# One x tile instead of two transposed on TensorE; the second comes first through the DMA transpose, behind the loads of Wk

## The chip, the cores and the metric

The kernel runs on one core of one Trainium2 chip. A core has five engines that run side by side: TensorE (PE, the matmuls; its weight loads stand in the profile as PEld), VectorE (DVE), ScalarE (ACT), GpSimd (POOL) and SyncE (SP, which here only issues transfers). Transfers run on 16 DMA engines that all queues share; SP and ACT each have a queue of their own. The metric is the device time of one execution in microseconds (us), and lower is better. A profile shows the span from the first instruction to the last; a little time lies around it.

## The reference

A block of linear attention with 32 heads of 20 columns, sequence length 2048, width 640, in bf16:

```python
B, S, D = 1, 2048, 640;  H = 32;  Dh = D // H
q, k, v = split(x @ wqkv)                  # wqkv: 640 x 1920, each part (B, H, S, Dh)
phi = lambda t: where(t > 0, t + 1, exp(t)) + 1e-6
pq, pk = phi(q), phi(k)
kv  = einsum("bhsd,bhse->bhde", pk, v)     # summed over the sequence, per head
z   = einsum("bhsd->bhd", pk)
num = einsum("bhqd,bhde->bhqe", pq, kv)
den = einsum("bhqd,bhd->bhq", pq, z)[..., None] + 1e-6
out = (num / den).reshape(B, S, D) @ wo
```

## The kernel before

The sequence is cut into 16 tiles of 128 rows, the width into 5 chunks of 128 columns. Wk is the middle third of `wqkv`; its 5 row chunks of 160 KB are `wk` chunks 0 to 4. The work goes in this order on TensorE: a few warm-up matmuls on constants; K = x Wk, tile by tile (line 293); the product of pk with x, from which kv is made with Wv later (line 317, "P"); Q in blocks of 512 rows (line 354), mixed with P; the small products that fold kv and Wo into one matrix; the denominators; the output (line 576).

A matmul needs x with its columns on the partitions. So there are two copies of x in SBUF: `xn`, rows on partitions, as it lies in memory (used by P and by the transposes), and `xT`, transposed (used by K and Q). `xT` is filled in two ways. Tiles below `NPE` are loaded into `xn` and turned on TensorE by `transpose_x`: five 128x128 transposes in two parts (chunks 0 and 1, then 2 to 4) into a PSUM bank each, copied out by VectorE (first part, line 212) and ScalarE (second part, line 209). All other rows come by DMA transposes (`load_xT`, line 189), one for each entry of `XCH` from number `NPE` on, all issued by SP. Before the change `NPE` is 2, and the entries used are rows 256 to 384, 384 to 640, 640 to 1024, 1024 to 1536 and 1536 to 2048: tile 2, tiles 3 and 4, 5 to 7, 8 to 11, 12 to 15.

One K tile is ten matmuls of 320 columns: two halves (`h`) of five chunks, accumulated in two PSUM banks (`k_half`). Four tiles use the eight banks in turn, so tile 4 needs the banks of tile 0. `k_phi` then runs one ScalarE exponential (line 306) and two VectorE operations (lines 308 and 311) for each tile.

`Plan` writes out one list of instructions for each engine, in the order of the program, and puts a semaphore wait ahead of an instruction where it reads what another engine or a transfer wrote. Nothing is reordered: an engine that waits holds up all that stands behind it. Loads go out in this order before the change (a letter and two numbers name a range of chunks or tiles: `w23` is `wk` chunk 2, `x12` is tile 1 of `xn`):

- SP: the left half of x tile 0, w01, w23, w34; then the five DMA transposes; then `load_rest`: Wq, x rows for tiles 2 to 7, 8 to 11, 12 to 15, ten pieces of Wv, three of Wo.
- ACT: the exponential's table, the right half of x tile 0, x12, w12, w45.

At the start TensorE takes tiles 0 and 1 together, chunk by chunk as Wk lands. The order is written out by hand at line 630: `k00a` is tile 0, chunk 0, first half; `t1b` is the second part of the transpose of tile 1; `k13` is tile 1, chunk 3, both halves. From tile 2 on each tile is done whole.

Of the kernel before, what the change touches and what calls it, by code (L numbers as in the profile page):

```python
# [84 lines left out]
def bass_standalone__linear_attn_block__prompt_kernel(nc, x, wqkv, wo, out):  # L85
# [4 lines left out]
    NT = S // 128  # L90
# [10 lines left out]
    with contextlib.ExitStack() as ctx:  # L101
# [43 lines left out]
        def two_banks(b, n=HALF, parts=128):  # L145
            return ps[0:parts, BK * b:BK * b + 2 * BK].rearrange(
                "p (g j) -> p g j", j=BK)[:, :, 0:n]

        def fold(ap, j=HALF):
            return ap.rearrange("p (g j) -> p g j", j=j)  # L150
# [26 lines left out]
                    band(bm[:, GT * t:GT * (t + 1)], [[-DH if lo else DH, 3], [0, DH]],  # L177
                         -64 * t if lo else DH - 1 + 64 * t, 1 if lo else -1, "bm")

        NPE = 2  # L180
        XCH = [(0, 128), (128, 256),
               (256, 384), (384, 640), (640, 1024), (1024, 1536), (1536, 2048)]

# [3 lines left out]
        def load_xT():  # L187
            for i, (a, b) in enumerate(XCH[NPE:]):
                P.add("sp", lambda e, a=a, b=b: e.dma_start_transpose(
                    xT[:, :].rearrange("p (c s) -> p c s", s=S)[:, :, a:b], x[0, a:b, :]),  # L190
                    writes=[("xT", NPE + i)], dma=True)

# [22 lines left out]
        def xT_keys(a, b, cs=range(NC_)):  # L215
            keys = []
            for i, (p, q) in enumerate(XCH):
                if p < b and a < q:
                    keys += [("xT", i)] if i >= NPE else sorted(
                        {("xT", i, 0 if c < 2 else 2) for c in cs})  # L220
            return keys

        def w_cols(dst, lo, hi, col, key, eng):
            P.add(eng, lambda e: e.dma_start(
                dst[:, 0:NC_ * D].rearrange("p (c n) -> p c n", n=D)[:, :, lo:hi],
                wqkv[:, col + lo:col + hi].rearrange("(c p) n -> p c n", p=128)),
                writes=[key], dma=True)

        def load_xn(a, b, eng):
            P.add(eng, lambda e: e.dma_start(  # L230
                xn[:, a * D:b * D].rearrange("p (t n) -> p t n", n=D),
                x[0, 128 * a:128 * b, :].rearrange("(t p) n -> p t n", p=128)),
                writes=[("xn", t) for t in range(a, b)], dma=True)

        def load_wk():
            tl = mybir.InstLoadActFuncSet(
                name=nc.get_next_instruction_name(),
                act_func_set_id=ACT_TABLE_SET_LN_EXP, ins=[], outs=[])
            P.add("act", lambda e: e.add_instruction(tl), writes=["table"])
            for eng, lo in (("sp", 0), ("act", HALF)):  # L240
                P.add(eng, lambda e, lo=lo: e.dma_start(
                    xn[:, lo:lo + HALF], x[0, 0:128, lo:lo + HALF]),
                    writes=[("xn", 0, lo)], dma=True)
            for eng, what in (("sp", "w01 w23 w34"), ("act", "x12 w12 w45")):
                for k in what.split():
                    a, b = int(k[1]), int(k[2])
                    if k[0] == "x":
                        load_xn(a, b, eng)
                    else:
                        P.add(eng, lambda e, a=a, b=b: e.dma_start(  # L250
                            wk[:, a * D:b * D].rearrange("p (c n) -> p c n", n=D),
                            wqkv[128 * a:128 * b, D:2 * D].rearrange("(c p) n -> p c n", p=128)),
                            writes=[("wk", c) for c in range(a, b)], dma=True)
# [3 lines left out]

        def load_rest():
            w_cols(wqn, 0, D, 0, "wqn", "sp")
            for a, b in ((2, 8), (8, 12), (12, 16)):  # L260
                load_xn(a, b, "sp")
            for g, n in ((0, 5), (5, 1)):
                f = min(GT, gsz[g])
                k = gsz[g] // f * n
                for d in range(NC_):
                    P.add("sp", lambda e, g=g, f=f, k=k, d=d: e.dma_start(
                        wv[:, 128 * NG * d:128 * NG * (d + 1)].rearrange(
                            "p (j f) -> p j f", f=64)[:, 2 * g:2 * g + k, 0:f],
                        wqkv[128 * d:128 * (d + 1), 2 * D + goff[g]:2 * D + goff[g] + k * f].rearrange(
                            "p (j f) -> p j f", f=f)),  # L270
                        writes=[("wv", i, d) for i in range(g, g + n)], dma=True)
            for t in range(2):
                P.add("sp", lambda e, t=t: e.dma_start(
                    wog[64 * t:64 * t + GT, 0:5 * D].rearrange("p (g n) -> p g n", n=D),
                    wo[0:5 * GW, :].rearrange("(g t p) n -> t p g n", t=2, p=GT)[t]),
                    writes=[("wog", g, t) for g in range(5)], dma=True)
            P.add("sp", lambda e: e.dma_start(
                wog[0:gsz[5], 5 * D:6 * D], wo[goff[5]:, :]),
                writes=[("wog", 5, 0)], dma=True)

        def warm(n, cols=BK):
            for _ in range(n):
                P.add("pe", lambda e: e.matmul(  # L283
                    bank(4, cols), nc.const_aps.tensor(1.0, [128, 128], BF16),
                    nc.const_aps.tensor(1.0, [128, cols], BF16), start=True, stop=True),
                    writes=[("bank", 4)])

        def k_half(st, h, cs=range(NC_)):
            b = 2 * (st % 4)

            def mm(e):
                for c in cs:
                    r = e.matmul(  # L293
                        bank(b + h, HALF),
                        xT[:, c * S + 128 * st:c * S + 128 * st + 128],
                        wk[:, c * D + HALF * h:c * D + HALF * (h + 1)],
                        start=(c == 0), stop=(c == NC_ - 1))
                return r
            P.add("pe", mm, reads=xT_keys(128 * st, 128 * st + 128, cs) + [("wk", c) for c in cs],
                  writes=[("bank", b + h)])  # L300

        def k_phi(st):
            b = 2 * (st % 4)
            banks = [("bank", b), ("bank", b + 1)]
            t = ek[st % 3]
            P.add("act", lambda e: e.activation(fold(t[:, :]), two_banks(b), ACTF.Exp),  # L306
                  reads=banks + ["table"], writes=[("ek", st % 3)])
            P.add("dve", lambda e: e.tensor_scalar(  # L308
                t[:, :], t[:, :], 1.0, 1e-6, ALU.min, ALU.add),
                reads=[("ek", st % 3)], writes=[("ek", st % 3)])  # L310
            P.add("dve", lambda e: e.scalar_tensor_tensor(  # L311
                fold(pk[:, st * D:(st + 1) * D]), two_banks(b), 0.0, fold(t[:, :]),
                ALU.max, ALU.add),
                reads=banks + [("ek", st % 3)], writes=[("pk", st)])
# [305 lines left out]

        pool_const()
        load_wk()
        load_xT()
        load_rest()
        warm(5)
        warm(1, 128)
        for part in range(2):
            transpose_x(0, part)
        warm(1)
        order = "k00a t1a k00b t1b k10 k01 k11 k02 k12 k03 k13 k04 k14"  # L630
        for k in order.split():
            st, part = int(k[1]), "ab".find(k[-1])
            if k[0] == "t":
                transpose_x(st, part)
            else:
                for h in range(2) if part < 0 else (part,):
                    k_half(st, h, (int(k[2]),))
        for st in range(2):
            k_phi(st)
        for st in range(2, NT):  # L640
            k_half(st, 0)
            k_half(st, 1)
            k_phi(st)
# [117 lines left out]
```

## Time and profile before

| | before |
|---|---|
| time of three runs, median (lowest to highest) | 99.58 us (99.29 to 100.04) |
| the profiled execution: its time | 99.56 us |
| the profiled execution: span | 98.3 us |
| TensorE busy | 95.1 us (97%) |
| VectorE, ScalarE, GpSimd busy | 63.7, 48.8, 4.7 us |
| K (line 293): 160 matmuls | 22.8 us |
| transposes on TensorE (line 200): 10 | 1.1% of the chain that ended last |
| first and last DMA transpose issued at | 2.65 and 11.60 us |
| Wq issued at, x for tiles 2 to 7 issued at | 15.00, 16.33 us |
| first Q matmul on the chain | 29.18 us |

Times inside the execution are microseconds from the start of the span. In a timeline a row is a run of equal instructions: start, length, engine, line, operation, what it writes and reads, count, and in brackets the idle time of its engine just before and what ended it. "SPq" and "ACTq" are the queues that issue transfers; the length there is that of the issue, not of the transfer. A row of transfers gives the size in KB and the time from the start of the issue to the landing. A busy TensorE can be one that runs slowly or overlaps: starts of successive matmuls tell its pace better than their durations, which overlap.

### The profile page before, as it was taken

The numbers are of one execution on the slowest core, as the hardware profiler recorded it, in microseconds if no ns is written. First come the engines' busy times: TensorE is split into PE (matmuls) and PEld (weight loads), VectorE is DVE, ScalarE is ACT, GpSimd is POOL, SyncE is SP. The second block draws the span as 40 slices with busy tenths as digits, with TensorE's granted clock in tenths as the row PEclk, the third lists the DMA queues.
The fourth block names the chain that finished last, engine by engine and source line by source line (L and its number), as shares of the span: only waits on it lengthen the run. The fifth ranks groups of instructions, "written<-read, shape, count | busy, mean of one in ns | idle before, by whom it ended". The sixth has DMA issues, their size and how long they took to land.

```text
span 98.3 us, 1814 instructions
## 1 busy us (share of the span) xinstructions
PE 95.1 (97%) x694; PEld 61.2 (62%) x699; DVE 63.7 (65%) x124; ACT 48.8 (50%) x93; POOL 4.7 (5%) x19
## 2 busy tenths in 40 slices
PE   6999999999999999999999999999999999999991
PEld 2467777777755444445687867655557677777771
DVE  5314998888899439997839836758999206272222
ACT  5116455544526120005806456796988765453532
POOL 6500000000000000000000520000000000000000
DMA  2999999999998294000340023313200335532334
GB/s 48 320 269 194 238 157 111 350 366 360 316 169 108 21 239 80 0 0 0 63 77 7 0 63 93 94 32 86 79 0 0 133 74 168 205 117 87 130 133 137
DMA packets 26369, 12.60 MB, mean 128 GB/s; under 512 B 18553, under 2 KB 26361, under 8 KB 26361
## 3 DMA queue, kind: packets, MB, share of 16 engines
q1 hardware_dynamic: 25640, 11.87, 50.2%
q10 hardware_dynamic: 720, 0.61, 1.9%
q8 instruction: 5, 0.08, 0.3%
q14 instruction: 4, 0.02, 0.1%
HBM read 5.90 MB, written 2.62 MB: 87 GB/s over the span
## 4 chain that ended last, share of the span: by engine, by line
PE 95%; ACT 2%; issue 0%
PE ps L293 23%; PE ps L576 22%; PE ps L354 22%; PE ps L317 21%; PE ps L283 3%; ACT w2g L483 2%; PE ps L445 1%; PE ps L544 1%; PE ps L200 1%; PE ps L472 1%; ACT osb L599 0%
## 5 line engine op out<-in xcount | busy, mean ns | idle before, releaser
L317 PE MATMUL ps<-pk,xn 128*128 128x480 bf16 (+1 forms) x160 | 23.2, 299 | 0.0
L293 PE MATMUL ps<-wk,xT 128*128 128x320 bf16 x160 | 22.8, 303 | 0.0
L354 PE MATMUL ps<-xT,wqn 128*128 128x512 bf16 x95 | 22.0, 379 | 0.4 <-issue 0.2
L576 PE MATMUL ps<-w2p,pq 128*128 128x320 bf16 (+2 forms) x170 | 22.1, 291 | 0.0
L293 PEld LDWEIGHTS ps<-wk,xT 128*128 128x128 bf16 x160 | 15.6, 98 | 6.8 <-DMA wk<-in_wqkv_dram 0.9
L576 PEld LDWEIGHTS ps<-w2p,pq 128*128 128x128 bf16 x170 | 15.9, 98 | 6.2 <-issue 0.2
L317 PEld LDWEIGHTS ps<-pk,xn 128*128 128x128 bf16 x160 | 13.6, 98 | 9.4 <-issue 0.3
L362 ACT ACTIVATE eq<-ps 128x512 bf16<-128x512 f32 x20 | 11.9, 597 | 13.8 <-PE ps L354 13.6
L354 PEld LDWEIGHTS ps<-xT,wqn 128*128 128x128 bf16 x100 | 11.5, 118 | 9.1 <-issue 0.3
L306 ACT ACTIVATE ek<-ps 128x640 bf16<-128x640 f32 x16 | 11.2, 704 | 10.7 <-PE ps L293 10.1
L599 ACT CAST osb<-ps 128x320 bf16<-128x320 f32 (+2 forms) x27 | 11.0, 413 | 9.7 <-PE ps L576 9.0
L311 DVE SCALAR_TENSOR_TENSOR pk<-ps,ek 128x640 bf16<-128x640 f32 x16 | 13.2, 825 | 0.5
L569 DVE TENSOR_TENSOR pq<-pq,rd 128x512 bf16<-128x512 bf16 x20 | 7.3, 418 | 4.2 <-DMA rd<-rdc 4.2
L375 DVE TENSOR_SCALAR eq<-eq 128x512 bf16<-128x512 bf16 x20 | 5.8, 288 | 5.9 <-ACT eq L362 5.8
L602 DVE CAST osb<-ps 128x320 bf16<-128x320 f32 (+1 forms) x7 | 3.2, 456 | 8.7 <-PE ps L576 8.7
L308 DVE TENSOR_SCALAR ek<-ek 128x640 bf16<-128x640 bf16 x16 | 5.2, 325 | 5.3 <-ACT ek L306 5.1
L366 ACT ACTIVATE rq<-ps 128x512 bf16<-128x512 f32 x13 | 7.7, 592 | 0.0
L339 ACT CAST pt<-ps 128x480 bf16<-128x480 f32 x4 | 2.2, 562 | 8.2 <-PE ps L317 8.1
L379 DVE TENSOR_TENSOR pq<-eq,rq 128x512 bf16<-128x512 bf16 x13 | 5.5, 426 | 1.1 <-ACT rq L366 0.7
L388 DVE TENSOR_TENSOR za<-pk 128x1280 f32<-128x1280 bf16 x4 | 5.8, 1482 | 0.0
L382 DVE SCALAR_TENSOR_TENSOR pq<-ps,eq 128x512 bf16<-128x512 f32 x7 | 4.8, 692 | 0.2
L388 DVE TENSOR_TENSOR za<-za 128x1280 f32<-128x1280 f32 x3 | 4.4, 1486 | 0.0
(37 smaller groups left out, 36.7 us busy)
## 6 DMA issues: line engine op xcount, KB each, us to landing
out_dram<-osb SPq DMA_DIRECT2D x15, 160.0 KB, 1.8
xn<-in_x_dram SPq DMA_DIRECT2D x2, 640.0 KB, 8.9
xn<-in_x_dram SPq DMA_DIRECT2D x1, 960.0 KB, 7.0
wqn<-in_wqkv_dram SPq DMA_DIRECT2D x1, 800.0 KB, 5.6
wv<-in_wqkv_dram SPq DMA_DIRECT2D x5, 150.0 KB, 5.1
wog<-in_wo_dram SPq DMA_DIRECT2D x2, 375.0 KB, 5.3
w2p<-w2g SPq DMA_DIRECT2D x10, 75.0 KB
rd<-rdc SPq DMA_DIRECT2D x8, 64.0 KB, 2.1
```

What stands on the lines that cost most here:

```text
L293: r = e.matmul(bank(b + h, HALF), xT[:, c * S + 128 * st:c * S + 128 * st + 128], wk[:, c * D + HALF * h:c * D + HALF * (h + 1)], start=(c ...
L306: P.add("act", lambda e: e.activation(fold(t[:, :]), two_banks(b), ACTF.Exp), reads=banks + ["table"], writes=[("ek", st % 3)])
L311: P.add("dve", lambda e: e.scalar_tensor_tensor(fold(pk[:, st * D:(st + 1) * D]), two_banks(b), 0.0, fold(t[:, :]), ALU.max, ALU.add), rea ...
L317: return e.matmul(bank(d // PB[h], PW[h], off=PW[h] * (d % PB[h])), xn[:, st * D + 128 * d:st * D + 128 * d + 128], pk[:, st * D + PO[h]:s ...
L354: r = e.matmul(bank(b), wqn[:, d * D:(d + 1) * D].rearrange("p (q c) -> p c q", c=NC_)[:, c, :], xT[:, d * S + BK * sbk:d * S + BK * (sbk ...
L362: P.add("act", lambda e: e.activation(t[:, :], bank(b), ACTF.Exp), reads=[("bank", b), "table"], writes=[("eq", i)])
L366: P.add("act", lambda e: e.activation(r[:, :], bank(b), ACTF.Relu), reads=[("bank", b), "table"], writes=[("rq", i)])
L375: P.add("dve", lambda e: e.tensor_scalar(t[:, :], t[:, :], 1.0, 1e-6, ALU.min, ALU.add), reads=[("eq", i)], writes=[("eq", i)])
L388: P.add("dve", lambda e: e.tensor_tensor(d_ap, a, b, ALU.add), reads=ra + rb, writes=[dst])
L569: P.add("dve", lambda e: e.tensor_tensor(v, v, rd[i][:, BK * h:BK * (h + 1)], ALU.mult), reads=[("rd", i, 2 * h), ("rd", i, 2 * h + 1), (" ...
L576: r = e.matmul(bank(b, hi - lo), pq[:, c * S + 128 * st:c * S + 128 * st + 128], w2p[:, c * D + lo:c * D + hi], start=(c == 0), stop=(c == ...
L599: P.add("act", lambda e: e.copy(osb[j][:, lo:hi], bank(b, hi - lo)), reads=[("bank", b)], writes=keys)
```

## The change

Only tile 0 is transposed on TensorE. The early load of tile 1 on ACT's queue and its five transposes and two copies go. The DMA transposes start one entry earlier, with rows 128 to 256, so SP issues six of them instead of five; they still stand behind SP's three pieces of Wk. Chunks 3 and 4 of Wk change queues: SP now loads w01, w23, w45, and ACT w12, w34. Tile 1 of `xn`, which P still needs, comes in `load_rest` together with tiles 2 to 7. On TensorE tile 0 alone goes chunk by chunk as Wk lands, both halves of a chunk together; tile 1 is done whole after it, like all the others.

```diff
-        NPE = 2
+        NPE = 1
         XCH = [(0, 128), (128, 256),
                (256, 384), (384, 640), (640, 1024), (1024, 1536), (1536, 2048)]
...
-            for eng, what in (("sp", "w01 w23 w34"), ("act", "x12 w12 w45")):
+            for eng, what in (("sp", "w01 w23 w45"), ("act", "w12 w34")):
...
             w_cols(wqn, 0, D, 0, "wqn", "sp")
-            for a, b in ((2, 8), (8, 12), (12, 16)):
+            for a, b in ((1, 8), (8, 12), (12, 16)):
                 load_xn(a, b, "sp")
...
-        order = "k00a t1a k00b t1b k10 k01 k11 k02 k12 k03 k13 k04 k14"
+        order = "k00 k01 k02 k03 k04"
         for k in order.split():
...
-        for st in range(2):
-            k_phi(st)
-        for st in range(2, NT):
+        k_phi(0)
+        for st in range(1, NT):
             k_half(st, 0)
             k_half(st, 1)
             k_phi(st)
```

## The prediction

> **What bounds the kernel now.** First the page: who is busy, and which engine the chain that ended last runs through.
>
> ```profile
> PE 95.1 (97%) x694; PEld 61.2 (62%) x699; DVE 63.7 (65%) x124; ACT 48.8 (50%) x93; POOL 4.7 (5%) x19
> ...
> PE 95%; ACT 2%; issue 0%
> ```
>
> TensorE is the chain: what its K stage ends later, the end comes later. Next the chain in order of time (start, length, what), where the change lies:
>
> ```profile
> 3.22 0.56 PE ps L200 x5
> 3.78 0.43 PE ps L283
> 4.20 0.44 PE ps L293
> 4.64 0.21 PE ps L200 x2
> 4.86 0.27 PE ps L293
> 5.12 0.32 PE ps L200 x3
> 5.44 21.66 PE ps L293 x158
> 27.10 2.03 PE ps L317 x10
> ```
>
> The five transposes of tile 1 (0.21 and 0.32) lie between the first K matmuls; from 5.44 on K runs in one piece. Then the K matmuls of two stretches, 4 to 5.7 and 5.9 to 27 (durations in ns, lowest/median/highest, then first and last start), and between them the one wait for Wk that the weight loads show:
>
> ```profile
> L293 PE MATMUL ps<-wk,xT x4: 391/458/474, 4.2 to 5.5; 128*128 128x320 bf16 x4
> ...
> 5.73 0.25 PEld L293 LDWEIGHTS ps<-wk,xT 128*128 128x128 bf16 x3 [0.34 <-DMA wk<-in_wqkv_dram]
> ...
> L293 PE MATMUL ps<-wk,xT x156: 299/299/309, 5.7 to 26.8; 128*128 128x320 bf16 x156
> ```
>
> From 5.73 on, 156 matmuls start without a stall, (26.8 - 5.73) / 155 = 0.136 us apart; a tile of ten takes 1.36. So before the change neither Wk nor a DMA transpose holds K up after 5.73. Last, the queue that feeds it: issues of DMA transposes on SP (the first two of x, and two of z later on, where the queue is empty), then the time from issue to landing of the same four in that order, then what the DMA engines moved from 3 to 6 us (last two columns: their busy share, GB/s):
>
> ```profile
> 2.65 1.33 SPq L189 DMA_TRANSPOSE xT<-in_x_dram  x1
> ...
> 4.03 2.13 SPq L189 DMA_TRANSPOSE xT<-in_x_dram  x1
> ...
> 47.21 1.35 SPq L423 DMA_TRANSPOSE zt<-zh  x1
> 48.60 1.27 SPq L423 DMA_TRANSPOSE zt<-zl  x1
> ```
>
> ```profile
> xT<-in_x_dram SPq DMA_TRANSPOSE x1, 4.6
> ...
> xT<-in_x_dram SPq DMA_TRANSPOSE x1, 5.0
> ...
> zt<-zh SPq DMA_TRANSPOSE x1, 2.7
> ...
> zt<-zl SPq DMA_TRANSPOSE x1, 2.8
> ```
>
> ```profile
> 3.00:4.00 1.00, 1.00 (x8) 0.53 (x6) 0.29 (x1) 0.19 (x1) 0.76 (x4) 1.00 0.97 324
> 4.00:5.00 1.00, 1.00 (x6) 0.61 (x6) 0.11 (x1) 0.29 (x1) 0.00 (x0) 1.00 1.06 373
> 5.00:6.00 1.00, 1.00 (x8) 0.54 (x7) 0.18 (x1) 0.48 (x1) 0.00 (x0) 1.00 1.27 321
> ```
>
> The first block landed at 2.65 + 4.6 = 7.25, the second (256 rows) at 4.03 + 5.0 = 9.03. The DMA engines are full from 3 us on.
>
> **The change, part by part.** The measure is when tile 1 starts. Before, 156 matmuls were left at 5.73. After tile 0 alone, 150 are left, so K ends at the same time if tile 1 starts at 5.73 + 6 x 0.136 = **6.55** and does not stall later. Each microsecond after that is lost whole: the rest of the chain is TensorE back to back, and the 1.49 us piece in which it waits for ScalarE's copies (line 483) follows a TensorE piece and moves with it.
>
> *Tile 0.* Its transposes, the warm-up matmul and w01 (1.24 + 2.9 = 4.14) stay, so it starts at 4.20. On ACT's queue w12 takes the place of x12 (1.23 + 3.1 = 4.33) and is there when chunk 0 is done. w23 landed at 1.70 + 3.8 = 5.5, and w34 takes the place of the old w12 (1.71 + 4.0 = 5.7). w45, now SP's third, landed there at 2.17 + 4.2 = 6.37 at the latest; two matmuls later tile 0 ends, by 6.37 + 0.05 + 0.27 = 6.69.
>
> *Block 1 (rows 128 to 256).* SP still issues three pieces of Wk first, so its issue stays at 2.65. Ahead of it 160 KB (x12) less share the DMA engines: at the mean of 324, 373 and 321 GB/s that is 163,840 B / 339 GB/s = 0.48 us. Nothing may be saved if SP's own queue sets the time, since it carries the same bytes as before ahead of the block. I take 0.35, nearer to the upper end because the DMA share is about 1 there: landing at 7.25 - 0.35 = 6.90. Tile 1 starts 0.05 later (w01's landing to its matmul took 0.06), at 6.95. Loss: 6.95 - 6.55 = **0.40 us**.
>
> This wait is new. Behind it on TensorE stand 150 K matmuls and all the rest; ScalarE's exponential of tile 1 and VectorE's two operations wait for it, but VectorE needs 0.33 + 0.82 us a tile against 1.36, and keeps up.
>
> *Blocks 2 and 3.* There is one block more in the queue. From the first landing (7.25) to the last (11.60 + 6.8 = 18.4) 1664 rows came in 11.15 us, 0.86 for 128 rows. Tile 2 is wanted at 6.95 + 1.36 = 8.31; block 2 lands at 6.90 + 0.86 = 7.76. Tile 3 is wanted at 9.67; block 3 lands at 9.03 - 0.35 + 0.86 = 9.54. No stall, by 0.13. Tile 5 is wanted at 12.39, its block landed at 6.20 + 5.0 = 11.2 and comes 0.51 later; tiles 8 and 12 have over a microsecond.
>
> The Trainium skill ("DMA: Bandwidth & Descriptors", Latency and other measured facts) gives 261 GB/s for a DMA transpose with a non-contiguous middle dimension, against 191 GB/s by the 0.86 here; by it block 3 would land at an estimated 9.31, and the sum would stay.
>
> *At nothing.* The 0.53 us of transposes taken off TensorE: the time goes into waiting for w23, w45 and block 1, as tile 0 ends before tile 1 can start; without that cover it is the gain of the third rival. One copy each on VectorE (0.29) and ScalarE (0.48): these sat idle 3.40 and 1.89 us before their next operation. The exponential of tile 0 comes earlier than 7.85. On SP, all that stands behind the transposes comes up to 0.86 later: Wq lands at 15.00 + 5.6 + 0.86 = 21.5, wanted at 29.18; x for tiles 1 to 7 at 16.33 + 7.0 + 0.86 and about 0.46 for 160 KB more (640 KB took 1.85), 24.7, wanted by P's second tile after 27.10 (without that cover P would stall by the difference); Wv (first used at 49.7) and Wo (54.7) have over 10 us. ACT's queue loses one issue of 0.46 us, and nothing waits for it after that.
>
> **Sum:** 99.56 + 0.40 = 99.96 us, against the profiled execution, which is the median (99.58) within its scatter. With 0.48 saved it is +0.27 (block 3 at 9.41, wanted at 9.54), with nothing saved +0.75: 99.83 to 100.31.
>
> **Rivals.**
>
> *Small blocks cost too much (slower).* The transposes of z, 128 x 640 with an empty queue, took 1.35 and 1.27 to issue and landed at 49.91 and 51.40, 1.49 apart; block 1 took 1.33 for 128 rows, and a later one 1.61 for 384. If blocks 1 and 2 land 1.49 apart and block 3 1.78 after that, as 9.03 follows 7.25, block 3 lands at 6.90 + 3.27 = 10.17 or, with nothing saved, at 10.52. Tile 3 would have to start at 6.55 + 2.72 = 9.27: a loss of 0.95 to 1.30, 100.5 to 100.9. Against it: the queue is full here, and two 128-row units landed as one block in 1.78.
>
> *TensorE stays slow longer (slower).* Early weight loads of the 512-column warm-up start 0.43 apart (1.20, 1.63, 2.06), 0.84 ns a column; K later takes 0.425. The page's clock column reads 1.00 throughout, so only the pace shows it; the first four K matmuls are still slow. The new start has gaps before chunk 2 and tile 1. If the pace doubles later, a tile costs up to 10 x 0.131 = 1.31 more, at least nothing: up to 101.3, taken at half to the whole, 100.6 to 101.3. Against it: until 5.3 us TensorE is as busy as before, and at the slow pace it would have fewer gaps.
>
> The Trainium skill ("TensorE: Matmul & The Clock Gate", Part 1) speaks against the change here: TensorE runs at half its clock until it has been busy over a free-running window of about 3.4 us. If one window failed, the next would by estimate end 3.4 us after the change of pace near 5.6, at 9.0: a loss near 1.0 on top of the forecast, 101.0.
>
> *Block 1 arrives with Wk (not slower).* Mechanism: with less beside it, block 1 lands soon after w45. It decides at a landing of 6.50, 0.75 earlier than before. If w45 gains 0.48, tile 0 ends at 5.89 + 0.32 = 6.21, and tile 1 follows: 0.34 won, 99.2; so 99.2 to 99.56. For it: the blocks of z landed 2.7 after issue. Against: 0.48 is all that the removed load can give. This is also the most that the change can win; over 1% would need something that no view shows.
>
> That the change does not do what it says, since block 1's time is not set by the load ahead, is the forecast's upper end.
>
> **How the numbers follow.** Forecast 0.42; small blocks 0.32; slow TensorE 0.13; block 1 early 0.10; something else 0.03. The predicted time is the forecast's, 99.96. The range is 99.4 to 101.0: it leaves out the better half of the third rival and the upper part of the slow one. 1%, 1.0 us, is about what a measurement of this kernel can tell from no change. Slower by more (over 100.56): two thirds of the small blocks (0.21), nearly all of the slow case (0.12), and 0.03: 0.36. Faster by over 1%: 0.03. Same: 0.61. The forecast itself is a small loss within that.
>
> **What would show it.** Right: the weight loads of line 293 wait 0.2 to 0.8 us for the DMA of xT once, and the first whole tile starts near 6.95; then 150 matmuls 0.136 apart and K ending near 27.5. A second wait for xT at tile 3, near 9.3, is the first rival; K matmuls of over 390 ns after 6 us are the second; no wait at tile 1 is the third. The forecast is wrong if block 1 lands later than 7.25, if P or Q waits for `xn` or Wq, or if the start of w01 moves.

## Result and profile after

The changed kernel is a little slower: 100.51 us (median of 9 runs, 100.09 to 101.94) against 99.94 us (99.29 to 102.31), ratio 1.0064, 95% interval 1.0041 to 1.0086. That is a loss of 0.4 to 0.9%, inside the 1% within which the forecast put it. The ratio and its interval leave out one slow execution of each kernel, so the ratio is not the quotient of the two medians. The profiled execution took 100.55 us with a span of 99.3 us; that of before 99.56 and 98.3. These two lie 0.99 us apart, more than the ratio says (that of before is faster than the median of its kernel, that of after slower): the traces show the cause, the ratio its size.

The page, busy times and the chain by engine:

```profile
PE 95.6 (96%) x694; PEld 60.5 (61%) x694; DVE 63.7 (64%) x123; ACT 48.3 (49%) x92; POOL 4.7 (5%) x19
...
PE 88%; DMA 5%; SPq 4%; issue 0%; ACT 0%
```

TensorE had 95% of the chain before; now 9% of it are SP's issues and a transfer. The chain in order of time (start, length, what) shows which transfer:

```profile
5.33 4.82 DMA xT<-in_x_dram
10.14 0.05 issue
10.19 17.83 PE ps L293 x130
28.02 2.02 PE ps L317 x10
```

It is the third DMA transpose, issued at 5.33 and landed at 10.14: 130 matmuls, tiles 3 to 15, hang on it. K ends at 28.02 instead of 27.10. The weight loads show every wait of K (start, length, operation, count, idle time before and what ended it):

```profile
4.39 0.66 PEld L293 LDWEIGHTS ps<-wk,xT 128*128 128x128 bf16 x4 [0.80 <-DMA wk<-in_wqkv_dram]
5.47 0.91 PEld L293 LDWEIGHTS ps<-wk,xT 128*128 128x128 bf16 x6 [0.42 <-DMA wk<-in_wqkv_dram]
6.62 1.20 PEld L293 LDWEIGHTS ps<-wk,xT 128*128 128x128 bf16 x10 [0.24 <-DMA xT<-in_x_dram]
8.02 1.20 PEld L293 LDWEIGHTS ps<-wk,xT 128*128 128x128 bf16 x10 [0.20 <-DMA xT<-in_x_dram]
10.19 1.88 PEld L293 LDWEIGHTS ps<-wk,xT 128*128 128x128 bf16 x15 [0.97 <-DMA xT<-in_x_dram]
```

Tiles 1, 2 and 3 each wait for their block. A weight load ends some time before its matmul does, so about 0.17 us of such a gap is no loss: by the starts of the matmuls tile 1 loses 0.07 us, tile 2 0.03 and tile 3 0.80. Before, there was no wait after 5.73. K's matmuls up to 6.1 and from 6.5 on, durations in ns (lowest/median/highest):

```profile
L293 PE MATMUL ps<-wk,xT x7: 330/461/474, 4.4 to 6.0; 128*128 128x320 bf16 x7
...
L293 PE MATMUL ps<-wk,xT x152: 299/299/310, 6.3 to 27.7; 128*128 128x320 bf16 x152
```

TensorE's pace doubles near 6.0, where before it was near 5.7, while tile 0 waits for Wk anyway. Issue and landing of the first three blocks:

```profile
2.65 1.33 SPq L189 DMA_TRANSPOSE xT<-in_x_dram  x1
4.02 1.26 SPq L189 DMA_TRANSPOSE xT<-in_x_dram  x1
5.33 1.33 SPq L189 DMA_TRANSPOSE xT<-in_x_dram  x1
```

```profile
xT<-in_x_dram SPq DMA_TRANSPOSE x1, 3.9
xT<-in_x_dram SPq DMA_TRANSPOSE x1, 4.0
xT<-in_x_dram SPq DMA_TRANSPOSE x1, 4.8
```

In the trace they land at 6.58, 7.98 and 10.14. Block 1 came earlier than forecast (6.90), blocks 2 and 3 later (7.76 and 9.54). The DMA engines were as full as before in all three of these stretches, but moved less in the third (321 GB/s before): 766 of its 813 packets were small ones of under 512 B, 467 of 631 before (last two columns: busy share, GB/s):

```profile
3.00:4.00 1.00, 1.00 (x8) 0.53 (x6) 0.29 (x1) 0.21 (x1) 0.76 (x4) 1.00 1.04 328
4.00:5.00 1.00, 0.79 (x4) 0.38 (x4) 0.00 (x0) 0.27 (x1) 0.00 (x0) 1.00 0.99 354
5.00:6.00 1.00, 1.00 (x6) 0.35 (x5) 0.00 (x0) 0.00 (x0) 0.00 (x0) 1.00 1.24 246
```

The whole loss is made in K. The time of an execution less the end of K is 72.46 us before (99.56 - 27.10) and 72.53 after (100.55 - 28.02), and the twelve profiled executions of the experiments, read in the same way, lie between 72.45 and 72.53.

### The profile page after: what moved, and what is told of

It reads as the page before. It is cut to its first block, busy times and chain, and to the rows that moved or that the text cites. A ratio compares the mean times of both kernels' runs of the same rounds, so it can differ in the third digit from the quotient of the medians.

```text
span 99.3 us, 1807 instructions
## 1 busy us (share of the span) xinstructions
PE 95.6 (96%) x694; PEld 60.5 (61%) x694; DVE 63.7 (64%) x123; ACT 48.3 (49%) x92; POOL 4.7 (5%) x19
## 4 chain that ended last, share of the span: by engine, by line
PE 88%; DMA 5%; SPq 4%; issue 0%; ACT 0%
PE ps L576 22%; PE ps L317 22%; PE ps L354 22%; PE ps L293 18%; DMA xT<-in_x_dram 5%; SPq L189 3%; PE ps L445 1%; PE ps L544 1%; SPq L250 1%; PE ps L472 1%; SPq L241 0%; ACT osb L599 0%
## 5 line engine op out<-in xcount | busy, mean ns | idle before, releaser
L354 PE MATMUL ps<-xT,wqn 128*128 128x512 bf16 x100 | 23.1, 379 | 0.0
```

The lines of the kernel that those rows point to most:

```text
L354: r = e.matmul(bank(b), wqn[:, d * D:(d + 1) * D].rearrange("p (q c) -> p c q", c=NC_)[:, c, :], xT[:, d * S + BK * sbk:d * S + BK * (sbk ...
```

## Experiments

Ratios are to the kernel before, run beside each experiment. Two theories at first: **S**, a DMA transpose has a fixed price beside its rows, so one block more makes block 3 late; **R**, rows alone count, and the late block 3 was chance.

### The changed kernel again

> The changed kernel once more, unaltered, for a second profile and a narrower ratio. Theory S (small blocks): a DMA transpose costs a fixed time beside its rows, so the one block more makes block 3 (rows 384 to 640) land over 3.2 us after block 1 in every execution; tile 3 then waits 0.5 to 1.0 us again, K ends near 28.0, ratio to the kernel before 1.005 to 1.009. Theory R (rows alone, 0.86 us for 128 rows; the late block 3 of the first profile was chance): block 3 lands 2.6 us after block 1, tile 3 waits under 0.1 us, K ends near 27.4, and the ratio is what the wait at tile 1 leaves, 1.001 to 1.004.

No edit. 100.39 us, ratio 1.0068 (1.0043 to 1.0093). Blocks 1 to 3 landed at 6.89, 8.13 and 9.84, so block 3 came 2.95 after block 1, between the two expectations; and block 4 came late as well. Its weight loads from 6.9 us on:

```profile
6.93 2.56 PEld L293 LDWEIGHTS ps<-wk,xT 128*128 128x128 bf16 x20 [0.51 <-DMA xT<-in_x_dram]
9.88 2.56 PEld L293 LDWEIGHTS ps<-wk,xT 128*128 128x128 bf16 x20 [0.39 <-DMA xT<-in_x_dram]
13.09 0.93 PEld L293 LDWEIGHTS ps<-wk,xT 128*128 128x128 bf16 x8 [0.65 <-DMA xT<-in_x_dram]
```

Tiles 1, 3 and 5 wait, tile 2 doesn't, and K ends at 28.20. Tile 3 waits in both executions; how long it waits, and that tile 5 waits too, differs between them.

### The price of a block by itself

```diff
-               (256, 384), (384, 640), (640, 1024), (1024, 1536), (1536, 2048)]
+               (256, 384), (384, 512), (512, 640), (640, 1024), (1024, 1536), (1536, 2048)]
```

> The kernel before with one edit: rows 384 to 640 come as two DMA transposes of 128 rows instead of one of 256, so the disputed cost stands alone. The first three blocks are then 128 rows each. S: they land 1.3 to 1.5 us apart (7.2, 8.6, 10.0), rows 512 to 640 some 0.9 us later than the 9.06 of before, and every later block comes 0.5 or more late; tile 3 is served earlier and tile 4 is wanted only at 10.63, so the time is the same or 0.1 us better, ratio 0.998 to 1.001. R: they land 0.86 apart (7.2, 8.1, 9.0), later blocks as before, ratio 0.998 to 1.001.

On the kernel before: 99.88 us, ratio 1.0001 (0.9979 to 1.0023). Issue of the first three blocks, all of 128 rows, and below the time to landing:

```profile
2.65 1.33 SPq L189 DMA_TRANSPOSE xT<-in_x_dram  x1
4.03 1.26 SPq L189 DMA_TRANSPOSE xT<-in_x_dram  x1
5.33 1.28 SPq L189 DMA_TRANSPOSE xT<-in_x_dram  x1
```

```profile
xT<-in_x_dram SPq DMA_TRANSPOSE x1, 4.8
xT<-in_x_dram SPq DMA_TRANSPOSE x1, 4.2
xT<-in_x_dram SPq DMA_TRANSPOSE x1, 3.8
```

They landed at 7.42, 8.27 and 9.17 in the trace, 0.85 and 0.90 apart: the price by rows, 0.86. S does not hold here, and one block more costs nothing in the time. A small block takes 1.3 us to issue, but issues run ahead of the transfers and don't set the landings here.

### One larger first block

```diff
-        XCH = [(0, 128), (128, 256),
-               (256, 384), (384, 640), (640, 1024), ...
+        XCH = [(0, 128), (128, 384),
+               (384, 640), (640, 1024), ...
```

> The changed kernel with rows 128 to 384 as one DMA transpose of 256 rows: as many blocks as before the change, the same rows. S, with 1.40 for a block of 128 rows and 1.85 to 2.16 for 256 (0.45 to 0.76 for each further 128 rows): the first block lands at 7.0 to 7.35, rows 384 to 640 by 8.9 to 9.5, tile 1 starts near 7.2, tile 3 near 9.95 without a wait; ratio 1.002 to 1.005, better than the changed kernel by 0.2 us. R: the first block lands at 6.58 + 0.86 = 7.44, tile 3 starts at 10.2, as late as in the changed kernel's profile; ratio 1.006 to 1.009.

On the changed kernel: 101.09 us, ratio 1.0133 (1.0090 to 1.0176). The first block landed at 7.55, where R put it (7.44), and there is one wait in K:

```profile
7.59 6.50 PEld L293 LDWEIGHTS ps<-wk,xT 128*128 128x128 bf16 x49 [1.44 <-DMA xT<-in_x_dram]
```

After it nothing stalls, and K ends at 28.15, as in the changed kernel: what the later blocks lose there, the first one loses here. The other runs of this kernel were slower than its profiled one (100.63 us), and why the ratio is above R's 1.006 to 1.009 was not seen.

### The early load of tile 1 kept

```diff
-            for eng, what in (("sp", "w01 w23 w45"), ("act", "w12 w34")):
+            for eng, what in (("sp", "w01 w23 w45"), ("act", "x12 w12 w34")):
...
-            for a, b in ((1, 8), (8, 12), (12, 16)):
+            for a, b in ((2, 8), (8, 12), (12, 16)):
```

> The changed kernel with the early load of x tile 1 (160 KB) kept on ACT's queue where it was before, w12 and w34 behind it; nothing waits for that load early. It prices the relief: with the DMA engines shared, block 1 lands 0.35 to 0.6 us later than in the changed kernel (6.9 to 7.2 instead of 6.58), blocks 2 and 3 likewise, and the ratio is 1.009 to 1.012. If SP's own queue sets block 1, its landing stays near 6.6 and the ratio stays at 1.006, unless w34, now third on ACT's queue, holds up tile 0.

101.66 us, ratio 1.0164 (1.0117 to 1.0211), worse than expected. Block 1 landed at 7.64, 1.06 later than in the changed kernel's profile, blocks 2 and 3 at 8.22 and 10.43, only 0.24 and 0.29 later. But most of the loss is something else: K's matmuls between 6.5 and 9.3 us (durations in ns).

```profile
L293 PE MATMUL ps<-wk,xT x12: 446/474/474, 6.2 to 9.1; 128*128 128x320 bf16 x12
```

They run at half pace, to near 9.6 us (the last slow one starts at 9.36). w01 had landed late, at 5.08, and TensorE's weight loads had been idle for 1.52 us before it. So a further theory, **C**: the pace doubles only after TensorE has been busy for a while, and idle time at the start puts it off.

### The same with the idle time filled

```diff
-        order = "k00 k01 k02 k03 k04"
+        order = "w w w w w k00 w w k01 w k02 w k03 w k04"    # w: warm(1, 256)
```

> The kernel with the early load of x tile 1 kept, which lost 1.6%, with warm-up matmuls of 256 columns added where TensorE stood idle there: five ahead of tile 0, two ahead of its chunk 1, one ahead of chunks 2, 3 and 4. In that kernel's profile K ran at half pace until 9.4 us. Theory C (the pace doubles only after TensorE has been busy for a while, and the idle 1.5 us before 5.1 put it off): with the gaps filled the pace doubles near 5.5 again, no K matmul is slow after 6.5, and the ratio falls from 1.016 to 1.008 to 1.011. If the moment of the doubling is chance, the ratio stays at 1.014 to 1.018, or the fillers add to it.

100.67 us, ratio 1.0086 (1.0056 to 1.0116), no overlap with the 1.0164 without fillers. K's matmuls between 6.5 and 9.3 us:

```profile
L293 PE MATMUL ps<-wk,xT x20: 299/299/299, 6.4 to 9.2; 128*128 128x320 bf16 x20
```

This is what C forecast. In the profile K starts as late as without the fillers (5.04 against 5.12), and the pace doubles near 6.1 instead of 9.6. Idle time may not be all of it: one of the six executions without fillers took 100.47 us, while the six with them lie between 100.57 and 100.81. What is left of the early load, 1.0086 against 1.0064, is small; their intervals overlap.

### Which waits make the loss

```diff
         def k_half(st, h, cs=range(NC_)):
+            xs = min(st, 1)        # in the third kernel: xs = 0
...
-                        xT[:, c * S + 128 * st:c * S + 128 * st + 128],
+                        xT[:, c * S + 128 * xs:c * S + 128 * xs + 128],
```

and the same in the tile's list of what it reads. First on the changed kernel:

> The changed kernel, but in K the tiles 2 to 15 use the transposed x of tile 1 in place of their own, so K waits for block 1 of the DMA transposes and for no later one; all loads go out as before, K's values are others. Theory L (later blocks): the loss is made by blocks 2 to 4 that land late now and then (tile 3 waited in the first profile, tiles 3 and 5 in the second). Then K ends 20.5 us after tile 1 starts, near 27.4 to 27.6, and the ratio falls from 1.0065 to 1.001 to 1.004. Theory F (the first wait is all): the ratio stays at 1.006.

99.99 us, ratio 1.0020 (0.9995 to 1.0045). One wait is left, and K runs through from there to its end at 27.66:

```profile
7.11 6.91 PEld L294 LDWEIGHTS ps<-wk,xT 128*128 128x128 bf16 x52 [0.58 <-DMA xT<-in_x_dram]
```

From the first matmul of tile 1 to the end of K it is 20.54 us here (7.12 to 27.66); 21.39 in the changed kernel (6.63 to 28.02) and 21.27 in its repetition (6.93 to 28.20). So the later blocks cost 0.73 to 0.85 us in those two executions. Block 1 came earlier in them, so K ends only 0.36 and 0.54 us later than here. Then on the kernel before:

> The same edit on the kernel before: tiles 2 to 15 use the transposed x of tile 1, so K waits for no DMA transpose at all. L, with the kernel before having at least 0.2 us of room at each block: ratio 0.998 to 1.000. If late blocks cost the kernel before something too in usual executions (its median of 99.9 lies above the 99.56 of its profile), the ratio is 0.993 to 0.997.

99.89 us, ratio 1.0012 (0.9983 to 1.0041): the kernel before loses nothing measurable to its DMA transposes. (Its profile is of an execution of 102.04 us, in which w01 landed at 5.19 and the pace doubled near 9.6.) Then the changed kernel without any wait for them:

> The changed kernel, but in K all tiles use the transposed x of tile 0, so K waits for no DMA transpose; all loads go out as before, K's values are others. Waiting only for block 1 the ratio was 1.002. Theory: the wait for block 1 makes up what was left, so tile 1 starts when tile 0 ends, near 6.4 to 6.6, K ends near 27.0 to 27.3 and the ratio is 0.997 to 1.000. Rival: what was left is not the block but the later end of tile 0 (chunks of Wk, slow pace); then the ratio stays at 1.001 to 1.003.

99.56 us, ratio 0.9963 (0.9937 to 0.9989); K ends at 26.83. With these the change can be taken apart, in ratios to the kernel before:

| K waits for | ratio | step |
|---|---|---|
| no DMA transpose | 0.9963 | -0.0037: transposes gone from TensorE, Wk earlier |
| block 1 alone | 1.0020 | +0.0057 |
| all blocks | 1.0064, 1.0068 | +0.0044 to +0.0048 |

The intervals of the first two rows don't overlap. Those of the last two do, by at most 0.0004, and there the traces back the step, by the later end of K (0.36 and 0.54 us).

The steps hold in this order only. In the first profile of the changed kernel K's end follows from the landing of block 3 alone (10.19 + 17.83 = 28.02), in the repetition from that of block 4 (tile 5 starts at 13.09, and nothing waits after it). Had tile 1 not waited there, K would by this have ended no sooner: the wait for block 1 is hidden behind the later ones. No run took away the wait for block 1 alone.

### The blocks ahead of the last chunk of Wk

```diff
-            for eng, what in (("sp", "w01 w23 w45"), ("act", "w12 w34")):
+            for eng, what in (("sp", "w01 w23"), ("act", "w12 w34 w45")):
```

> The changed kernel with the last chunk of Wk moved from SP to the end of ACT's queue, so SP issues the DMA transposes one issue (0.48 us) earlier, no longer behind all of Wk. If the place behind Wk sets when the blocks land, all of them land 0.3 to 0.5 us earlier, w45 lands near 6.3, tile 1 starts near 6.5, and the ratio falls from 1.0066 to 1.002 to 1.004. If the blocks and Wk only share the same DMA engines, block 1 lands at 6.5 to 6.9 as it did, w45 later than 6.3, and the ratio is 1.005 to 1.009.

100.27 us, ratio 1.0034 (1.0009 to 1.0058), as the place behind Wk would have it; but its other signs did not come. In the profile block 1 landed at 7.24, later than before the edit, and w45 at 6.66, not 6.3:

```profile
7.29 6.77 PEld L293 LDWEIGHTS ps<-wk,xT 128*128 128x128 bf16 x51 [0.47 <-DMA xT<-in_x_dram]
```

Nothing waits after that, as blocks 3 to 5 landed at 9.51, 12.00 and 14.95 instead of 10.14, 12.82 and 15.64. By the ratios half of the loss is regained, and by the profile at the blocks further back; but the intervals of the two kernels overlap (1.0009 to 1.0058, 1.0041 to 1.0086), so the gain is not shown.

### Attempts at something faster

```diff
+            for eng, lo in (("sp", 0), ("act", HALF)):
+                P.add(eng, lambda e, lo=lo: e.dma_start(
+                    wk[:, lo:lo + HALF], wqkv[0:128, D + lo:D + lo + HALF]),
+                    writes=[("wk", 0, lo)], dma=True)
-            for eng, what in (("sp", "w01 w23 w34"), ("act", "x12 w12 w45")):
+            for eng, what in (("sp", "w12 w34"), ("act", "x12 w23 w45")):
```

and in K each half waits for its own half of chunk 0.

> An attempt at a version that beats both: the kernel before with chunk 0 of Wk cut into two column halves, one on each queue right behind the halves of x tile 0 (SP then w12 and w34, ACT x12, w23, w45). Tile 0's first half waits only for its own half, so K should start at 3.7 to 3.9 instead of 4.2 to 4.4. If the start is what holds K, the ratio is 0.995 to 0.998; if TensorE's slow pace or the last chunk of Wk sets the end of tiles 0 and 1, it is 0.998 to 1.002.

A miss: 101.03 us, ratio 1.0095 (1.0058 to 1.0131). In the profile (100.34 us) K started at 4.08, hardly earlier, and x12, now ACT's third load, landed at 5.54 instead of 4.34; the transposes of tile 1 waited for it, with K behind them.

```profile
5.58 0.11 PEld L200 LDWEIGHTS ps<-ident,xn 128*128 128x128 bf16 x2 [1.40 <-DMA xn<-in_x_dram]
```

```diff
-            for eng, what in (("sp", "w01 w23 w34"), ("act", "x12 w12 w45")):
+            for eng, what in (("sp", "w01 w12 w34"), ("act", "x12 w23 w45")):
```

> An attempt at a version that beats both: the kernel before with chunks 1 and 2 of Wk changing queues (SP w01, w12, w34; ACT x12, w23, w45). In every profile SP's second piece lands 0.2 us before ACT's second, and the one wait for Wk that the kernel before shows is for w12. If that wait sets K's end, K ends 0.2 us earlier: ratio 0.997 to 0.999. If the pace of TensorE hides it: 0.999 to 1.002.

99.75 us, ratio 0.9985 (0.9959 to 1.0011). In the profiled execution, the fastest of its twelve, K ends at 26.79, 0.31 earlier than in the profile of before, and the wait for w12 shrank from 0.34 to 0.15:

```profile
5.42 8.68 PEld L293 LDWEIGHTS ps<-wk,xT 128*128 128x128 bf16 x65 [0.15 <-DMA wk<-in_wqkv_dram]
```

With the two fillers on top:

> The same, and one warm-up matmul of 256 columns ahead of tile 0 and one ahead of its chunk 1, so that TensorE is idle less before its pace doubles. If late executions of the kernel before (101 us and more) come from the pace doubling late, they become rarer and the ratio is that of the swap alone or up to 0.002 better; if the fillers only stand in the way, it is 0.001 to 0.003 worse.

99.70 us, ratio 0.9981 (0.9950 to 1.0012). Both are faster than the changed kernel; neither is told apart from the kernel before.

## Why the prediction held, and which step did not

Way, size and range held: 0.40% was forecast, 0.64% (0.41 to 0.86) measured. Step by step:

- **K's end is the measure, one to one.** Right: 72.45 to 72.53 us lie between it and the time in every profile read.
- **Tile 0 ends by 6.69, before block 1.** Right: its last matmul started at 6.42, and block 1 landed at 6.58. w45 landed at 5.93, near the 5.89 that the third rival took.
- **Block 1 lands at 6.90.** Right on the mean: 6.58, 6.89, 7.07 and 6.66 in four executions with the same loads (the changed kernel twice, and the two with waits removed), 6.80, 0.41 earlier than the 7.21 of before, where 0.35 was taken; but 7.21 is one execution. The loss from this wait with all that was gained before it was put at 0.40 us; the kernel that waits for block 1 alone has 0.20% (-0.05 to 0.45), and in its profile tile 1 starts at 7.12 and K ends 0.56 us later than in that of before.
- **"No stall, by 0.13" at tile 3.** Wrong, and this is the step that failed. It let blocks 2 and 3 come 0.35 earlier with block 1 and added 0.86 for the one block more. But only block 1 came earlier. In the same four executions block 2 landed at 7.95 to 8.20 and block 3 at 9.84 to 10.21, 10.06 on the mean, 0.5 later than the 9.54 forecast. With the 0.86 added and nothing taken off, the sum would have been 7.21 + 0.86 = 8.07 and 9.06 + 0.86 = 9.92. Nor do the later blocks follow block 1 when it is late: in the two kernels with the early load kept it came at 7.64 and 7.13, block 2 at 8.22 and 8.27, block 3 at 10.43 and 10.31. Block 4, put at 11.2 + 0.51, came at 12.66 to 13.04. So tile 3 waits (0.80 us in the first profile), and in the repetition tile 5 too. The 0.86 itself was a mean over 1664 rows: two neighbouring blocks came 0.85 and 0.90 apart in one kernel and 1.40 and 2.16 (the latter for 256 rows) in another. A margin of 0.13 us on a mean was no margin. Behind the wait for block 1 the later blocks add 0.44 to 0.48%, where nothing was put down.
- **At nothing.** Right: Wq landed at 21.62 and x for tiles 1 to 7 at 24.76, as forecast (21.5 and 24.7), and neither Q nor P waits for them. The transposes taken off TensorE, with Wk earlier, are worth 0.37% once nothing waits for a DMA transpose, and the third rival said 0.34 us; the waits hide that.
- **The rivals.** *Small blocks* gave the second wait at tile 3 that was named as its sign, block 3's landing almost to the number (10.17; it was 10.14) and the loss between the two profiles (0.95; it was 0.99), for a reason that the split block speaks against. *Slow TensorE* did not happen in the profiles of this kernel; in the one with the early load kept it did, and filling the gap undid it. *Block 1 early* held for half the way: it landed at 6.58 in one execution, next to its 6.50, and the later blocks took the gain back.

So the total held partly by luck. The wait for block 1, put at 0.40, has 0.20% with an interval that includes 0.40, and the later waits, put at nothing, have more than 0.4%. And the forecast's path is not the one that ended last: in the first profile K's end hangs on block 3, not on block 1.

What stays open is why the blocks behind the first do not move up with it. The split shows that it is not the number of blocks; the kernel with the transposes ahead of w45, whose third block came at 9.51 in the one profile, speaks for their place among the loads. The changed kernel's trace shows what the wait for block 3 looks like. From 6 to 10 us all packets are SP's and under 512 B, so only the DMA transposes move data (last two columns: busy share, GB/s):

```profile
8.00:9.00 1.00, 1.00 (x10) 0.71 (x9) 0.75 (x2) 0.70 (x1) 0.00 (x0) 1.00 1.26 239
9.00:10.00 1.00, 0.56 (x5) 0.18 (x2) 0.96 (x2) 0.41 (x1) 0.00 (x0) 1.00 1.02 74
```

The DMA engines are busy in both stretches, but 967 packets start in the first and 290 in the second: over 16 engines that is by estimate 1.26 x 16 us / 967 = 0.021 us for a packet, then 1.02 x 16 us / 290 = 0.056 us. Before, the slow stretch was 8 to 9 us (110 GB/s), and 9 to 10 us moved 291. So block 3 waits neither for its issue nor for another load, but for slow packets of the transposes; what makes them slow no run tells.

## What to carry to other kernels

Where work is moved from a full engine to a queue, ask not only when its first piece arrives but how much room each later piece has: in the profile of before, every DMA transpose landed at least 0.2 us before it was wanted, and with the change they landed later than K wanted them. A mean rate over a long queue does not price the next piece; take the spread of single landings and want a margin larger than it. To find what a wait costs, let the consumer read data that is already there and leave all transfers as they are: two such runs showed that a loss of 0.6% is made by these waits. Such terms hold in the order in which the waits are taken away, since a later wait can hide an earlier one.

## What the runs showed of the hardware that was not expected

- TensorE's pace doubles at a moment that differs between executions: near 5.7 us in the profile of before and 6.0 in that of after, but before 4.2 us in that of the changed kernel without waits for DMA transposes, with the same loads. Idle time can put it off much further. In the kernel with the early load kept, with weight loads idle for 1.52 us before 5.1 us, it doubled near 9.6; with K starting as late but the gap filled, near 6.1. The ratios differ by 0.8% (1.0164 against 1.0086). The late doubling needs no changed loads: the profile of the kernel before with its waits removed shows it too, near 9.6 after weight loads idle for 1.65 us.
- The Trainium skill ("TensorE: Matmul & The Clock Gate", Part 1) tells of a free-running window of about 3.4 us in which TensorE must be busy. From 6.0 in one execution to 9.6 in another is 3.6 us, which is near it, but no run here measures the window. The profile's clock column reads 1.00 all the while; only the durations (446 to 474 ns against 299) show the pace.
- DMA transposes of 128 x 640 land 0.58 to 1.40 us after the one ahead of them (0.58 with the early load kept, 1.40 in the changed kernel), with issues of 1.26 to 1.33 us in both.
